# Tile 0 of x loaded on ScalarE's DMA queue in a fused attention and gated MLP kernel

## The chip, the cores and the metric

The kernel runs on one core of a Trainium2 chip. A core has TensorE (matmuls), VectorE, ScalarE and GpSimd (elementwise work and reductions), and SyncE, which here only issues DMAs. ScalarE can issue DMAs too, on a queue of its own. The metric is the time of one execution on the device, in microseconds (us); less is better.

## The reference

A block with two residual steps on x of shape 1 x 2048 x 448, in bf16:

```python
x = A_x
h = x + _A_ref(_layernorm(x), A_wqkv, A_w_phi, A_wo)
h2 = h + _B_ref(_layernorm(h), B_w_gate, B_w_up, B_w_down)

# _A_ref: 16 heads of 28
qkv = x @ wqkv                       # split into q, k, v by head
pq, pk = q @ w_phi, k @ w_phi        # one 28 x 28 matrix per head
phi_q = concat(softmax(pq), softmax(-pq)); phi_k likewise
kv = phi_k^T @ v;  z = sum of phi_k over the sequence
o = (phi_q @ kv) / (phi_q . z + 1e-6);  return o @ wo

# _B_ref: inner width 1792
return (sigmoid(x @ w_gate) * (x @ w_up)) @ w_down
```

The second input named x (B_x) is not used.

## The kernel before

The sequence is cut into 16 tiles of 128 rows; tile t of x holds rows n = t of every 16, so that each of the 128 partitions reads one run of 896 bytes per tile. A tile is normalized (bst: statistics, agg: mean and variance, pow1: the reciprocal root, xn: the normalized tile) and turned so that the model width lies on the partitions (xT: through TensorE for tiles 0 to 3, by a transposing DMA for the others). The per-head matrices w_phi are not applied to q and k: they are multiplied into the weights beforehand ("folds", w2m). For the fold of the key weights the kernel loads them in two halves (ld_k0 with row blocks 0 and 1, ld_k2 with 2 and 3), transposes each block on TensorE (wT0 to wT3), copies it out (wTe, the first two on ScalarE, the last two on VectorE), and multiplies it with Wphi, a matrix with the heads' blocks on its diagonal (w2m0, line 627). Wphi is cleared by VectorE (bd0, line 444) and then filled by four small DMAs on ScalarE's queue (wphi0 to wphi3), which wait for the clearing. Every fold reads all of Wphi. The folded weights are copied out by ScalarE (w2e0).

After that come the projections of keys and values per tile (pp and vv for pairs of the first four tiles, pv for one tile later), exponentials on ScalarE, the sums over the sequence, the query side, the output projection, the second normalization and the gated MLP, whose 14 blocks of inner width are interleaved with what is left of the attention.

The order of the work is written out by hand: for each engine a string of step names (ORDER, lines 243 to 312), which that engine runs strictly in this order. A step waits on semaphores for the steps on other engines that it depends on. For the step names that matter here the orders begin:

```
SyncE:   x1 x0 ld_k0 x2 ld_k2 x4 x6 ld_v0 x10 ld_v2 x8 x12 ld_q1 ...
ScalarE: wphi3 wphi2 wphi1 wphi0 kvzones wTe0 wTe1 xT1e xT0e w2e0_0 ...
TensorE: warm0 wT0 wT1 xT1 warm1 .. warm3 xT0 warm4 wT2 wT3 w2m0_0 warm5 w2m0_2 w2m0_1 w2m0_3 warm6 .. warm8 xT3 ppa0 ppb0 xT2 warm9 vva0 ...
VectorE: zero steps bd0 wopad0 wopad1 mask2 bst1 agg1 bst0 agg0 xn1 xn0 bst3 bst2 agg3 wTe2 agg2 wTe3 ...
GpSimd:  epsl0 v1ones neghalf epsr0 ident0 ident pow1_1 pow1_0 pow1_3 phipad nm1_3 xn3 pow1_2 pow1_4 xn2 ...
```

The "warm" steps are matmuls of zeros whose result nobody reads. x0 and x1 load one tile each (112 KB); the other names x2, x4, ... load two tiles each (224 KB). All plain loads are recorded at one line (439, the helper load), so the traces show them by their destination: x_sb, wk_sb, wv_sb, Wphi.

Of the kernel before, what the change touches and what calls it, by code (L numbers as in the profile page):

```python
# [18 lines left out]
class Graph:  # L19
# [109 lines left out]
    def emit(self, nc):  # L129
# [112 lines left out]

ORDER = {
# [6 lines left out]
    ),  # L250
    "act": (
# [103 lines left out]
def build(nc, A_x, A_wqkv, A_w_phi, A_wo, B_w_gate, B_w_up, B_w_down, out):  # L355
# [4 lines left out]
    x_t = A_x[0].rearrange("(p n) d -> p n d", p=P)  # L360
# [5 lines left out]
    with ExitStack() as es:  # L366
        def sb(name, shape, d=dt.bfloat16):
            return es.enter_context(nc.sbuf_tensor(name, shape, d))
# [5 lines left out]
        par = sb("par", [P, 2])  # L374
        st2 = sb("st2", [P, 2, 9], f32)
        mv2 = sb("mv2", [P, 2, 2], f32)
        x_sb = sb("x_sb", [P, NT, D])
# [60 lines left out]
        def load(name, dst, src, w, kb, r=(), eng="sp", many=None):  # L438
            return op(eng, name, lambda e: e.dma_start(dst, src), r=r, w=w, dma="in" if eng == "sp" else "ain",  # L439
                      nring=(48 if eng == "sp" else 8) if many is None else 0, kb=kb, many=many)  # L440
# [48 lines left out]


        def xload(a, b):
            return load("x%d" % a, x_sb[:, a:b, :], x_t[:, a:b, :], [("x", t) for t in range(a, b)], (b - a) * 112)

        def kload(a, b):
            load("ld_k%d" % a, wk_sb[:, a:b, :], A_wqkv[a * GP:b * GP, D:2 * D].rearrange("(kt p) n -> p kt n", p=GP),
# [13 lines left out]
        for a, b in ((0, 1), (1, 2), (2, 4), (4, 6), (6, 8), (8, 10), (10, 12), (12, 14), (14, 16)):  # L509
            xload(a, b)  # L510
# [95 lines left out]
        for kt in range(KT):  # L606
            b = (0, 1, 4, 5)[kt]
# [435 lines left out]
```

## Time and profile before

| what | value |
|---|---|
| time, median of 3 runs | 201.93 us (201.68 to 201.96) |
| the profiled execution: its time | 201.4 us |
| the profiled execution: its span | 199.5 us |
| granted TensorE clock over the span | 1.0 |
| busy: TensorE, VectorE, ScalarE, GpSimd | 98%, 64%, 50%, 35% of the span |
| chain that ended last, by engine | TensorE 92%, VectorE 3%, DMA 2%, SyncE's queue 1%, issue 1% |
| HBM read, written | 8.34 MB, 1.84 MB |

The span runs from the first to the last instruction of the core; the time around it belongs to the start and end of the execution. PE is TensorE's matmul row and PEld its weight loads, DVE is VectorE, ACT ScalarE, POOL GpSimd. SPq and ACTq are the rows of the DMA-issuing instructions of SyncE and ScalarE. L and a number is a line of the kernel. An arrow in a tile's name reads "written from": psum<-Wphi,WkT is a matmul of those two into PSUM.

### The profile page before, as it was taken

The numbers are of one execution on the slowest core, as the hardware profiler recorded it, in microseconds if no ns is written. First come the engines' busy times: TensorE is split into PE (matmuls) and PEld (weight loads), VectorE is DVE, ScalarE is ACT, GpSimd is POOL, SyncE is SP. The second block draws the span as 40 slices with busy tenths as digits, with TensorE's granted clock in tenths as the row PEclk, the third lists the DMA queues.
The fourth block names the chain that finished last, engine by engine and source line by source line (L and its number), as shares of the span: only waits on it lengthen the run. The fifth ranks groups of instructions, "written<-read, shape, count | busy, mean of one in ns | idle before, by whom it ended". The sixth has DMA issues, their size and how long they took to land.

```text
span 199.5 us, 5929 instructions
## 1 busy us (share of the span) xinstructions
PE 194.7 (98%) x2528; PEld 114.3 (57%) x2528; DVE 126.8 (64%) x309; ACT 100.0 (50%) x213; POOL 69.5 (35%) x107
## 2 busy tenths in 40 slices
PE   7999999999989999999999999999999999999995
PEld 2835555666557788886555444444555555555553
DVE  6999999978889876286558775246232522353224
ACT  3869899899795776356232443223323212222210
POOL 4689968733543456353303146100210000000000
DMA  6995925478941573213102204203020000003103
GB/s 153 341 128 124 86 56 133 114 228 275 347 60 34 135 114 55 53 37 75 40 17 64 58 3 92 43 0 97 3 53 3 0 0 3 0 0 96 45 3 92
DMA packets 32866, 16.26 MB, mean 82 GB/s; under 512 B 25096, under 2 KB 31944, under 8 KB 32840
## 3 DMA queue, kind: packets, MB, share of 16 engines
q1 hardware_dynamic: 32336, 15.86, 35.3%
q8 instruction: 20, 0.33, 0.7%
q10 hardware_dynamic: 504, 0.03, 0.2%
q14 instruction: 6, 0.05, 0.1%
HBM read 8.34 MB, written 1.84 MB: 51 GB/s over the span
## 4 chain that ended last, share of the span: by engine, by line
PE 92%; DVE 3%; DMA 2%; SPq 1%; issue 1%
PE psum L338 87%; PE psum L960 3%; DMA wk_sb<-in_A_wqkv_dram 2%; PE psum L627 1%; SPq L439 1%; PE psum L536 1%; DVE c_sb L808 1%; DVE st L833 1%; PE psum L550 0%; DVE b_sb L805 0%; DVE hn_pad L855 0%; DVE xnT L543 0%; PE psum L611 0%; DVE x_sb L835 0%; DVE rsm L802 0%
## 5 line engine op out<-in xcount | busy, mean ns | idle before, releaser
L338 PE MATMUL psum<-xnT,wg_sb 64*128 64x512 bf16 (+1 forms) x490 | 95.1, 333 | 0.3 <-DVE xnT L543 0.3
L338 PE MATMUL psum<-xnT,wu_sb 64*128 64x512 bf16 (+1 forms) x490 | 95.0, 333 | 0.1
L914 ACT ACTIVATE sg_sb<-psum 128x512 bf16<-128x512 f32 (+1 forms) x70 | 35.6, 515 | 75.6 <-PE psum L338 75.2
L920 DVE TENSOR_TENSOR hhT<-sg_sb,psum 128x512 bf16<-128x512 bf16 (+1 forms) x44 | 29.2, 674 | 46.6 <-ACT sg_sb L914 46.0
L338 PEld LDWEIGHTS psum<-xnT,wg_sb 64*128 64x128 bf16 x490 | 44.7, 94 | 20.3 <-DVE hhT L920 0.8
L338 PEld LDWEIGHTS psum<-xnT,wu_sb 64*128 64x128 bf16 x490 | 44.6, 94 | 14.0 <-PE psum L338 0.9
L338 PE MATMUL psum<-wd_sb,hhT 64*128 64x448 bf16 x392 | 43.8, 349 | 0.0
L338 PEld LDWEIGHTS psum<-wd_sb,hhT 64*128 64x128 bf16 x392 | 20.9, 94 | 16.8 <-DVE x_sb L840 0.3
L338 PE MATMUL psum<-wv_sb,xnT 64*128 64x448 bf16 x112 | 22.2, 351 | 0.1
L338 PE MATMUL psum<-Wk,xnT 64*128 64x448 bf16 x112 | 22.1, 350 | 0.1
L814 POOL TENSOR_TENSOR o_pad<-c_sb,rden 128x448 bf16<-128x448 bf16 x12 | 11.2, 935 | 26.5 <-DVE rden L810 26.0
L687 POOL TENSOR_TENSOR phi<-hhT,rs 128x896 bf16<-128x896 bf16 x10 | 16.9, 1704 | 2.9 <-DVE rs L683 1.7
L677 DVE TENSOR_REDUCE ss<-hhT 128x32 f32<-128x896 bf16 x16 | 17.0, 1063 | 0.3
L725 ACT ACTIVATE eq<-psum 120x1024 bf16<-120x1024 f32 x16 | 15.8, 1031 | 0.9 <-PE psum L338 0.9
L338 PE MATMUL psum<-xnT,Wq 64*120 64x512 bf16 x112 | 14.8, 384 | 0.1
L967 DVE SCALAR_TENSOR_TENSOR x_sb<-psum,x_sb 128x448 bf16<-128x448 f32 (+2 forms) x17 | 9.7, 594 | 7.5 <-PE psum L338 5.1
L919 ACT CAST xn_pad<-psum 128x256 bf16<-128x256 f32 x26 | 9.4, 375 | 6.4 <-PE psum L338 5.8
L338 PE MATMUL psum<-wo_o,oT 64*128 64x448 bf16 x49 | 11.5, 349 | 0.0
L338 PE MATMUL psum<-wo_e,oT 64*128 64x448 bf16 x49 | 11.5, 349 | 0.0
L920 POOL TENSOR_TENSOR hhT<-sg_sb,xn_pad 128x256 bf16<-128x256 bf16 x11 | 7.6, 694 | 11.1 <-ACT xn_pad L919 6.9
L338 PEld LDWEIGHTS psum<-Wk,xnT 64*128 64x128 bf16 x112 | 7.7, 94 | 5.5 <-PE psum L338 1.0
L805 DVE TENSOR_TENSOR b_sb<-psum,qq 128x464 bf16<-128x464 f32 x16 | 10.1, 634 | 0.7 <-PE psum L338 0.4
(112 smaller groups left out, 244.0 us busy)
## 6 DMA issues: line engine op xcount, KB each, us to landing
out_dram<-x_sb SPq DMA_DIRECT2D x15, 112.0 KB, 1.8
x_sb<-in_A_x_dram SPq DMA_DIRECT2D x7, 224.0 KB, 4.5
wd_sb<-in_B_w_down_dram SPq DMA_DIRECT2D x7, 224.0 KB, 7.5
wg_sb<-in_B_w_gate_dram SPq DMA_DIRECT2D x3, 448.0 KB, 4.5
wu_sb<-in_B_w_up_dram SPq DMA_DIRECT2D x3, 448.0 KB, 4.7
wv_sb<-in_A_wqkv_dram SPq DMA_DIRECT2D x2, 224.0 KB, 4.9
wk_sb<-in_A_wqkv_dram SPq DMA_DIRECT2D x2, 196.0 KB, 3.5
wo_e<-in_A_wo_dram SPq DMA_DIRECT2D x1, 336.0 KB, 3.2
```

The costliest lines, as they stand in the source:

```text
L338: p = e.matmul(o, lhsT=w, rhs=r, start=st, stop=sp, tile_position=(row, 0))
L439: return op(eng, name, lambda e: e.dma_start(dst, src), r=r, w=w, dma="in" if eng == "sp" else "ain", nring=(48 if eng == "sp" else 8) if ...
L677: op("dve", "ss%d" % t, lambda e: e.tensor_reduce(ss[:, s, :].rearrange("p (b h) -> p b h", h=2), eks.rearrange("p b (d h) -> p b h d", h= ...
L687: return e.tensor_tensor(phi[:, sp, :, :, :].rearrange("p b a n -> p (b a) n")[:, :, 0:56].rearrange("p b (d h) -> p b d h", h=2), eks.rea ...
L725: op("act", "eq%d_%d%s" % (c, i, "pm"[sg]), lambda e, sg=sg: e.activation(eq[c][:, sg, 2 * i:2 * i + 2, :].rearrange("p g n -> p (g n)"), ...
L805: op("dve", "b%d" % t, lambda e: e.tensor_tensor(h3(b_sb), OMv[:, :, :, 0:EV], h2(qq)[:, :, :, None].to_broadcast([P, NB, 8, EV]), ALU.mul ...
L814: return e.tensor_tensor(o_pad[:, t % NO, off:off + D].rearrange("p (h d) -> p h d", h=H), c_sb[:, t % NS, :, 0:DH], rden[:, t % NS, :][:, ...
L914: op("act", "sig" + nm, lambda e: e.activation(sg_sb[:, k, 0:N], bk(bg)[:, 0:N], ACT.Sigmoid), r=[B(bg)], w=[("sg", k)])
L919: op("act", "uc" + nm, lambda e: e.copy(up, bk(bu)[:, 0:N]), r=[B(bu)], w=[ub])
L920: op(("pool", "dve") if nm in UCOPY else "dve", "hh" + nm, lambda e: e.tensor_tensor(hhT[(t0 // 4) % NHH][:, ff, ns], sg_sb[:, k, 0:N], up ...
L960: p = e.matmul(bk(b)[:, lo:hi], lhsT=hb[:, ff, TS(t)], rhs=wd_sb[:, ff, lo:hi], start=ff == 0, stop=ff == FT - 1)
L967: op("dve", "fin%d%s" % (t, nm), lambda e: e.scalar_tensor_tensor(out=h_sb[:, t, lo:hi], in0=bk(b)[:, lo:hi], scalar=1.0, in1=h_sb[:, t, l ...
```

## The change

Step x0 is taken out of SyncE's order and put at the head of ScalarE's, ahead of the four Wphi loads. All other steps keep their order on every engine. The helper for x's loads passes on the engine that the order names, and a load that is not on SyncE uses ScalarE's set of semaphores.

```diff
 ORDER = {
     "sp": (
-        "x1 x0 ld_k0 x2 ld_k2 x4 x6 ld_v0 x10 ...
+        "x1 ld_k0 x2 ld_k2 x4 x6 ld_v0 x10 ...
     ),
     "act": (
-        "wphi3 wphi2 wphi1 wphi0 kvzones wTe0 ...
+        "x0 wphi3 wphi2 wphi1 wphi0 kvzones wTe0 ...
...
         def xload(a, b):
-            return load("x%d" % a, x_sb[:, a:b, :], x_t[:, a:b, :], [("x", t) for t in range(a, b)], (b - a) * 112)
+            return load("x%d" % a, x_sb[:, a:b, :], x_t[:, a:b, :], [("x", t) for t in range(a, b)], (b - a) * 112, eng=Graph.engine("x%d" % a))
```

18 rows, old and new, of the table ORDER are left out of this document.

## The prediction

> **What bounds the kernel now.** I read the page's busy times first, then the chain of waits in order of time, then the first 14 us of the timeline. The change touches only the loads at the start, so two things matter: what sets the pace after the start, and which wait at the start hands a delay on to it.
>
> ```profile
> PE 194.7 (98%) x2528; PEld 114.3 (57%) x2528; DVE 126.8 (64%) x309; ACT 100.0 (50%) x213; POOL 69.5 (35%) x107
> ...
> 0.72 0.39 SPq L439
> 1.18 0.41 SPq L439
> 1.64 0.42 SPq L439
> 2.10 0.46 SPq L439
> 2.60 3.82 DMA wk_sb<-in_A_wqkv_dram
> 6.47 0.62 PE psum L611 x8
> 7.09 0.20 PE psum L627 x4
> 7.29 0.45 PE psum L536 x8
> 7.73 0.59 PE psum L627 x12
> 8.32 1.12 PE psum L536 x20
> 9.44 0.22 PE psum L550 x4
> ...
> 63.72 55.53 PE psum L338 x800
> 119.30 72.45 PE psum L338 x706
> ```
>
> The columns of the chain are start, length and what the time went to. SyncE's first four issues (x1, x0, ld_k0, x2) stand on it, then the fifth, ld_k2, from its issue at 2.60 to its landing at 6.42; from 6.47 on TensorE runs piece on piece: the last weight transposes (L611), the folds (L627), warm-up matmuls (L536), xT3 (L550). The long later pieces have no wait inside. So whatever TensorE loses or gains by 10 us is still there at 199.5 us. x0 itself is not on the chain as a transfer, only as an issue of 0.41.
>
> **The neighbours of that chain.** The timeline's rows, start and length again, the idle time before it in brackets:
>
> ```profile
> 1.18 3.57 PE L536 MATMUL psum<-zero 128*128 128x512 bf16 x9 [1.18 <-DVE zero L443]
> 1.20 0.24 DVE L444 MEMSET Wphi<- 112x224 uint32 x1
> 1.47 1.90 ACTq L439 DMA_DIRECT2D Wphi<-in_A_w_phi_dram  x4
> 2.84 0.63 DVE L557 BATCH_NORM_STATS2 st<-x_sb 128x6 f32<-128x448 bf16 x1 [0.29 <-DMA x_sb<-in_A_x_dram]
> 3.09 0.93 SPq L439 DMA_DIRECT2D x_sb<-in_A_x_dram  x2
> 3.50 0.20 DVE L558 BATCH_NORM_AGGREGATE mv<-st 128x2 f32<-128x9 f32 x1
> 3.62 0.59 DVE L557 BATCH_NORM_STATS2 st<-x_sb 128x6 f32<-128x448 bf16 x1
> 4.76 0.62 PE L611 MATMUL psum<-ident,wk_sb 112*112 112x112 bf16 x8
> 6.47 0.62 PE L611 MATMUL psum<-ident,wk_sb 112*112 112x112 bf16 x8 [0.31 <-DMA wk_sb<-in_A_wqkv_dram]
> 6.88 0.25 PEld L627 LDWEIGHTS psum<-Wphi,WkT 112*128 112x128 bf16 x4
> 6.92 0.39 DVE L543 COPY WkT<-psum 112x448 bf16<-112x448 bf16 x1
> 7.52 0.65 PEld L627 LDWEIGHTS psum<-Wphi,WkT 112*128 112x128 bf16 x12
> 8.37 0.77 POOL L588 TENSOR_SCALAR xn_pad<-x_sb,nm,rst 128x512 bf16<-128x512 bf16 x1
> 9.28 0.39 PE L550 MATMUL psum<-ident,xn_pad 128*128 128x128 bf16 x4
> 10.34 2.26 POOL L588 TENSOR_SCALAR xn_pad<-x_sb,nm,rst 128x512 bf16<-128x512 bf16 x3
> 11.27 0.40 PE L550 MATMUL psum<-ident,xn_pad 128*128 128x128 bf16 x4
> ```
>
> Three strands meet on TensorE: the key weights (ld_k0, ld_k2), the four small Wphi loads that ScalarE issues and every fold needs, and the statistics of x on VectorE and GpSimd that end in xT3 and xT2.
>
> **The change part by part.**
>
> *x0 off SyncE.* One issue of 0.41 goes; with its gap, 1.18 to 1.64, every later SyncE entry up to the first wait on work is issued 0.46 earlier. ld_k0 gains nothing by that: the first transposes start at 4.76, just when the nine warm-up matmuls end (1.18 + 3.57 = 4.75). ld_k2 can gain at most the wait of 0.31 in front of the second transposes. That gain has cover over it: the third fold group's operand comes from the copy on VectorE at 6.92 (end 7.31), which stands in VectorE's own order behind the statistics, so of the loads at 7.52 no more than 0.2 is left; xT3 waits for the normalized tile on GpSimd (8.37 + 0.77 = 9.14, against 9.28), and xT2 for the first of three tiles (10.34 + 2.26/3 = 11.09, against 11.27). What is left at xT2 is below 0.18; less a hand-over of about 0.05 (ld_k2 lands at 6.42, TensorE starts at 6.47), I take 0.1. Value of this part alone: -0.1 us, bounds -0.2 and 0.
>
> *x0 onto ScalarE.* ScalarE's first work is the Wphi issue at 1.47, when the clearing of Wphi (1.20 + 0.24) is done. An issue there lasted
>
> ```profile
> L439 ACTq DMA_DIRECT2D Wphi<-in_A_w_phi_dram x4: 338/418/632, 1.5 to 3.0; - x4
> ```
>
> 338 to 632 ns. Begun at about 0.72, as on SyncE, x0's issue ends by 1.35 at the latest of these, ahead of 1.47. So ScalarE pays nothing: cover is the clearing of Wphi. Should the start be late or the issue over 0.75, the excess moves all four Wphi issues, one for one.
>
> *x0 beside x1.* x1's statistics start the moment x1 lands (2.84, idle 0.29 ended by the DMA). x0's start at 3.62, straight behind VectorE's own aggregate (3.50 + 0.20), so an earlier x0 is worth nothing. But its 112 KB now travel beside x1's rather than behind. The windows' rows end in the rate in GB/s:
>
> ```profile
> 2.00:2.50 0.50, 0.50 (x3) 0.22 (x2) 0.35 (x2) 0.00 (x0) 0.23 (x1) 1.00 0.81 226
> 7.50:9.50 2.00, 2.00 (x41) 1.99 (x38) 2.00 (x8) 1.85 (x5) 1.83 (x4) 1.00 1.08 368
> ```
>
> At 368 GB/s, 114,688 bytes take 0.31. So x1 lands 0 to 0.31 later; I take 0.2. All of the VectorE and GpSimd strand moves with it, up to xT3 and xT2, where it has about 0.1 of slack: on its own 0 to +0.2 at the end, best value +0.1. It runs parallel to the next part, so the larger counts, not the sum.
>
> *Wphi against the SyncE stream.* This is the term I forecast by. Wphi's loads carry 6.1 KB each, but what do they wait for? The second queue (q10) carries only them; the DMA view gives packets of the whole run, then of 0 to 3.38, 5.5 to 6.5 and 6 to 6.5 us, and then the landing time (last number, us after issue) of the two loads issued around the last Wphi, ld_k2 and x4:
>
> ```profile
> q10 hardware_dynamic: 504, 0.03, 0.2%
> ...
> q10 hardware_dynamic: 119, 0.01, 3.2%
> ...
> q10 hardware_dynamic: 47, 0.00, 3.1%
> ...
> q10 hardware_dynamic: 1, 0.00, 0.1%
> ...
> x_sb<-in_A_x_dram SPq DMA_DIRECT2D x1, 224.0 KB, 4.4
> wk_sb<-in_A_wqkv_dram SPq DMA_DIRECT2D x1, 196.0 KB, 3.8
> ```
>
> All Wphi issues are over at 3.37 (1.47 + 1.90). Yet 47 of 504 packets start after 5.5, one after 6.0: over two us in a queue of its own that has nothing else in it. The last Wphi (issued 3.0) therefore moves about in order of issue among SyncE's loads, between ld_k2 (issued 2.60, landed 6.42) and x4 (issued 3.09, landed 3.09 + 4.4 = 7.49). It must have landed by 6.88, when the first fold loads its weights without a wait of its own, so in 6.42 to 6.88.
>
> After the change SyncE is one slot ahead and ScalarE is not: x4 is issued at 2.60, in ld_k2's old place, and the last Wphi at 3.0 falls behind x4. It then lands about when x4 does: 7.49 less what the stream gains. That gain is 0 if the DMA engines are full from the first load on, 0.46 if the whole issue slot is won: 7.03 to 7.49. Between the ends I take the middle, 7.26, since the rate of 226 against 368 shows that the engines are neither idle nor full at 2 us. The first fold moves from 6.88 to 7.26, +0.38; bounds +0.15 and +0.61. Nothing absorbs it: from L627 at 7.09 to xT3 at 9.44 TensorE has piece on piece, then the key projections, whose results release ScalarE's exponentials. Late next are those, and VectorE's sums of them.
>
> The Trainium skill ("DMA: Bandwidth & Descriptors", "Queues, rings and completion order") says that each DMA engine takes turns between the queue rows that have work, a packet at a time. By that rule Wphi would not stand behind x4 and this term would be 0, leaving the first part's -0.1. The packets after 5.5 us do not look like turns taken with a queue that has little in it, so I go by them.
>
> *The rest.* xT4 onwards and the weight loads are issued on waits for other work or for TensorE, and follow TensorE; the four transposing loads ld_q start 0.46 earlier behind the same loads, and the folds for q that use them stand in TensorE's order behind the key projections. Cost nothing. SyncE's final waits count the same loads.
>
> *Sum.* Larger of +0.38 (fold) and +0.1 (x1), with the -0.1 gone because the fold, not ld_k2, now ends last: +0.38. The profiled execution took 201.4 around a span of 199.5; it becomes 199.88 and 201.8. It lies 0.53 under the median of the runs, 201.93; against that the forecast is 201.93 + 0.38 = **202.3 us**, slower by 0.19%.
>
> **Rivals.**
>
> *The fold does not wait (other side).* Place: the first fold at 6.88. If queues take turns, or ScalarE's issues go faster once x0 was first (632 falls to 338 and the last Wphi goes out at 2.7), Wphi lands by 6.88 and ld_k2's lead shows: 201.93 - 0.1 = 201.8, at best 0.31 + a little, 201.6. It decides once the last Wphi lands under 6.88. For it: two queues, 6.1 KB each. Against: the late packets. The rule of the Trainium skill's page named above would bring this case about.
>
> *x1 is held up and the fold is not.* x1 0.31 late, less 0.1 of slack: 202.1. For it: x1's landing is waited for at 2.84. Against: the rate of 226 leaves room.
>
> *Everything late together.* x0's issue starts late on ScalarE and pushes Wphi, or the stream gains nothing: +0.6 and more, 202.6 to 202.8. For it: the first ScalarE issue was the longest. Against: nothing precedes it there.
>
> *The change is hidden.* x1 unhurt, fold and GpSimd strand both at their old times: 201.9.
>
> **How the numbers follow.** Fold waits as forecast 0.50 (own range 202.0 to 202.6), everything late 0.12, x1 only 0.10, faster side 0.20, hidden 0.08. What a measurement of this kernel tells from no change is about 0.2%, 0.4 us: 201.53 to 202.33. Slower by more: about half of the first case, most of the second, and shares of tail, 0.42. Faster by more: only the end of the faster side, 0.12. The rest, 0.46. Range: 201.6 to 202.8, from the faster side's best to the late end, leaves out about 2 in 10.
>
> **What would show it.** In the changed profile: x0 as ScalarE's first DMA near 0.72; ld_k2 issued near 2.10 and x4 near 2.60; second-queue packets still moving after 6.5 us; a wait in front of L627 and its first weight load near 7.26; xT3 near 9.7 (9.28 + 0.38). Wrong if the first fold loads at 6.9 or before, if x1's statistics start much after 3.1, or if Wphi's first issue starts after 1.5. Wrong in the other way if the front moves as forecast and a later stage gives it back.

## The result and the profile after

The changed kernel takes 202.42 us (median of 16 runs, 202.14 to 202.88), the kernel before 201.83 us (median of 16, 201.43 to 202.59): 0.59 us or 0.29% slower, ratio 1.0029, 95% interval 1.0019 to 1.0039. The profiled execution of the changed kernel took 202.61 us with a span of 200.7 us, so it lies 0.19 above its median, while that of before lies 0.43 below its own (201.4 against 201.83). The gap of 1.2 us between the two traces is therefore twice the gap of the medians; causes have to be read from several traces.

The chain of waits of the changed kernel in order of time (start, length, what):

```profile
0.72 0.40 SPq L439
1.18 0.41 SPq L439
1.64 0.45 SPq L439
2.13 5.08 DMA wk_sb<-in_A_wqkv_dram
7.26 0.62 PE psum L611 x8
7.88 0.28 issue
8.15 0.36 PE psum L627 x4
8.51 0.45 PE psum L536 x8
9.55 1.12 PE psum L536 x20
10.67 0.22 PE psum L550 x4
...
64.93 55.53 PE psum L338 x800
120.51 72.45 PE psum L338 x706
```

One issue is gone from SyncE's part and ld_k2 goes out at 2.13 instead of 2.60, as announced. But its transfer takes 5.08 instead of 3.82: issued 0.47 earlier, it lands 0.79 later. A new gap of 0.28 stands ahead of the first fold (L627), and everything after is the old chain, moved by 1.2: the piece of 55.53 us began at 63.72 before and begins at 64.93 now. The middle and the end of the kernel neither gave anything back nor lost more.

The timeline's rows that answer to those of before:

```profile
0.72 0.41 ACTq L439 DMA_DIRECT2D x_sb<-in_A_x_dram  x1
1.47 1.88 ACTq L439 DMA_DIRECT2D Wphi<-in_A_w_phi_dram  x4
2.61 0.93 SPq L439 DMA_DIRECT2D x_sb<-in_A_x_dram  x2
3.50 0.63 DVE L557 BATCH_NORM_STATS2 st<-x_sb 128x6 f32<-128x448 bf16 x1 [0.96 <-DMA x_sb<-in_A_x_dram]
7.26 0.62 PE L611 MATMUL psum<-ident,wk_sb 112*112 112x112 bf16 x8 [0.44 <-DMA wk_sb<-in_A_wqkv_dram]
8.15 0.36 PE L627 MATMUL psum<-Wphi,WkT 112*128 112x112 bf16 x4 [0.28 <-DMA Wphi<-in_A_w_phi_dram]
11.08 2.27 POOL L588 TENSOR_SCALAR xn_pad<-x_sb,nm,rst 128x512 bf16<-128x512 bf16 x3
12.49 0.40 PE L550 MATMUL psum<-ident,xn_pad 128*128 128x128 bf16 x4
```

ScalarE issues x0 at 0.72 and Wphi at 1.47, unchanged. x1's statistics (L557) start at 3.50 instead of 2.84, with 0.96 of idle time that x1's DMA ended. The fold waits 0.28 for Wphi by name. xT2 stands at 12.49 instead of 11.27.

The windows show the transfers themselves: the last number is GB/s, the first pair the stretch. Before, then after:

```profile
2.00:2.50 0.50, 0.50 (x3) 0.22 (x2) 0.35 (x2) 0.00 (x0) 0.23 (x1) 1.00 0.81 226
2.50:3.50 1.00, 1.00 (x4) 0.38 (x3) 0.68 (x2) 0.10 (x1) 0.00 (x0) 1.00 0.95 211
3.50:5.00 1.50, 1.49 (x8) 0.51 (x7) 1.25 (x4) 1.48 (x2) 1.04 (x2) 1.00 0.99 278
```

```profile
2.00:2.50 0.50, 0.50 (x3) 0.22 (x2) 0.35 (x2) 0.00 (x0) 0.23 (x1) 1.00 0.64 143
2.50:3.50 1.00, 1.00 (x4) 0.39 (x3) 0.05 (x1) 0.12 (x1) 0.00 (x0) 1.00 1.13 351
3.50:5.00 1.50, 1.50 (x5) 0.53 (x4) 1.43 (x4) 1.46 (x2) 0.56 (x1) 1.00 0.98 188
```

With two loads going out together the first half microsecond moves less, 143 against 226, not more. The next one makes up for it, and from 3.5 to 5.0 the stream is slower again. Over the three microseconds together these rates come to about 0.70 MB against 0.74 before, so SyncE's lead brought no more bytes.

### The profile page after: what moved, and what is told of

Same layout as the page of the kernel before. It is cut to its first block, busy times and chain, and to the rows that moved or that the text cites. A ratio compares the mean times of both kernels' runs of the same rounds, so it can differ in the third digit from the quotient of the medians.

```text
span 200.7 us, 5929 instructions
## 1 busy us (share of the span) xinstructions
PE 195.6 (97%) x2528; PEld 114.3 (57%) x2528; DVE 126.9 (63%) x309; ACT 100.0 (50%) x213; POOL 69.6 (35%) x107
## 4 chain that ended last, share of the span: by engine, by line
PE 92%; DVE 3%; DMA 3%; issue 1%; SPq 1%
PE psum L338 86%; PE psum L960 3%; DMA wk_sb<-in_A_wqkv_dram 3%; PE psum L627 1%; PE psum L536 1%; SPq L439 1%; DVE c_sb L808 1%; DVE st L833 1%; PE psum L550 0%; DVE b_sb L805 0%; DVE hn_pad L855 0%; DVE xnT L543 0%; PE psum L611 0%; DVE x_sb L835 0%; DVE rsm L802 0%
```

## The experiments

The theory at the start was the forecast's: the last Wphi load falls behind x4, and the fold waits. Rival one: x1 is held up by x0 beside it. Rival two: the whole stream ran late in that trace by chance. The experiments stand in three groups, each with its own runs of the kernel before, with medians of 201.67, 201.70 and 201.78. In kernels with an added load, line numbers behind it are one higher (L612 is L611).

**The changed kernel twice more.** Nothing is altered.

> The changed kernel once more, unaltered, for a second trace and a time beside the kernel before. In the first two traces the first fold loaded its weights at 6.88 before and 8.12 after (+1.24), while the medians of the runs differ by 0.59 us. Theory (the last Wphi load lands behind x4, and the fold waits for it): the second trace shows the fold waiting again, its weight load between 7.2 and 8.1, and a shift at the end of the same size; time ratio 1.002 to 1.004. Rival one (x1 is held up by x0 beside it): x1's statistics start at 3.1 or later again and the fold is late because everything behind them is. Rival two (the whole stream of loads happened to run late in that one trace): x1's statistics start near 2.85 and the second half of the key weights lands before 6.4 this time.

> The changed kernel unaltered, a third trace. In the first the fold waited 0.28 for Wphi, in the second not at all; in both the key weights' second half landed at 7.2 to 7.4 although it was issued 0.47 earlier than before. If that lateness belongs to the change: it lands after 7.0 again and the first fold loads its weights after 7.6. If it was chance: it lands at 6.9 or before. The fold waits for Wphi or not, either way; ratio 1.002 to 1.005.

Measured: 202.35 us, ratio 1.0033 (1.0021 to 1.0045), and 202.29 us, ratio 1.0029 (1.0016 to 1.0041). Rows of the second trace's timeline, then of the third's:

```profile
3.58 0.63 DVE L557 BATCH_NORM_STATS2 st<-x_sb 128x6 f32<-128x448 bf16 x1 [1.03 <-DMA x_sb<-in_A_x_dram]
7.42 0.62 PE L611 MATMUL psum<-ident,wk_sb 112*112 112x112 bf16 x8 [0.53 <-DMA wk_sb<-in_A_wqkv_dram]
7.83 0.25 PEld L627 LDWEIGHTS psum<-Wphi,WkT 112*128 112x128 bf16 x4
```

```profile
3.56 0.63 DVE L557 BATCH_NORM_STATS2 st<-x_sb 128x6 f32<-128x448 bf16 x1 [1.02 <-DMA x_sb<-in_A_x_dram]
6.96 0.62 PE L611 MATMUL psum<-ident,wk_sb 112*112 112x112 bf16 x8
7.85 0.36 PE L627 MATMUL psum<-Wphi,WkT 112*128 112x112 bf16 x4 [0.27 <-DMA Wphi<-in_A_w_phi_dram]
```

x1's statistics start at 3.50, 3.58 and 3.56 in the three traces: that is the change and not chance, and rival two is out. The fold waits for Wphi in two of three, by 0.28 and 0.27; in the other, ld_k2 came so late (7.38 by the chain) that Wphi was there first. The fold's weights are loaded at 8.12, 7.83 and 7.82, against 6.88 in the first trace of the kernel before and 7.12 in the second, which follows. The third expectation left ld_k2 after 7.0 or by 6.9; it landed at about 6.95 (2.15 + 4.8), between the two.

**The kernel before once more.** Nothing is altered.

> The kernel before once more, unaltered, for a second trace of its first 14 us. If x1's landing at 2.82 is what this kernel does and not chance: x1's statistics start within 0.1 of 2.84, and the key weights' second half lands within 0.4 of 6.43. Ratio 0.999 to 1.001.

Measured: 201.86 us against 201.70, ratio 1.0008 (1.0000 to 1.0017). x1's statistics start at 2.86, ld_k2's transposes at 6.72 and the fold's weights at 7.12. The 0.25 between the two traces of one kernel has to do with TensorE: the nine warm-up matmuls took 3.57 in the first and 4.02 in the second, where TensorE then ran without a gap up to the fold. So 0.16 us is what two series of one kernel can differ by here, and the 0.5 to 0.7 us of the change is well above it.

**x4 back at its place.**

```diff
-        "x1 ld_k0 x2 ld_k2 x4 ...
+        "x1 ld_k0 x2 ld_k2 pad0 x4 ...
+        load("pad0", junk[:, 0, 0:64], x_t[:, 0, 0:64], [("junk", 0)], 16)
```

The small load of 16 KB takes a slot, so x4 and every SyncE load behind it goes out at its old time.

> The changed kernel with one more small load (16 KB) in SyncE's order between ld_k2 and x4, so that x4 is issued at its old place, near 3.05, behind the last Wphi; x0 stays on ScalarE. Theory: the last Wphi lands ahead of x4 again, the fold does not wait, and most of the loss goes: ratio to the kernel before 0.999 to 1.001. Rival one (x1 held up beside x0): nothing changes there, ratio stays 1.002 to 1.004, x1's statistics start after 3.1. Rival two: no change either.

Measured: 202.01 us, ratio 1.0016 (1.0007 to 1.0026), 0.34 under the changed kernel of the same group; the runs (201.82 to 202.29) barely touch its runs (202.26 to 202.61). That lies between the two expected ratios. Its chain:

```profile
0.72 2.86 DMA x_sb<-in_A_x_dram
...
3.60 0.64 DVE st L558
...
5.27 0.70 POOL rst L567
...
9.08 0.78 POOL xn_pad L589
...
9.90 0.40 PE psum L551 x4
```

ld_k2, issued at the same 2.13 as in the changed kernel, now takes 4.3 to land instead of 4.8 to 5.2, and the fold's weights are loaded at 7.12. No packet of Wphi moves after 6.5 us, although x0 still stands ahead of Wphi on ScalarE's queue; so that place alone does not make the fold wait. The chain has moved to the other strand: x1's landing, 2.86 after its issue, its statistics, GpSimd, xT3. So moving up x4 and what follows it is one cause, and x1 beside x0 stands behind it as a second.

**Only x0 beside x1, SyncE's other loads as before.**

```diff
-        "x1 ld_k0 x2 ld_k2 x4 ...
+        "x1 pad0 ld_k0 x2 ld_k2 x4 ...
```

> The changed kernel with the small load (16 KB) in x0's old place in SyncE's order, so that SyncE's loads from ld_k0 on are issued at the times of before, and only x0 beside x1 is left of the change. Theory: Wphi keeps its place between ld_k2 and x4, ratio 0.999 to 1.001. Rival one: x1 lands up to 0.31 later and the ratio stays at 1.001 to 1.003. Rival two: no forecast, within 0.2% of the changed kernel.

> The changed kernel with the small load in x0's old place once more: SyncE's other loads as before, only x0 beside x1 is left. The first time three of twelve runs were near 204.1 and the interval was wide (1.003 to 1.007), with the others about 202.2. If x0 beside x1 costs about what the first trace shows (x1's statistics 0.41 later): ratio 1.001 to 1.003, the statistics start after 3.1.

Measured: 202.27 us, ratio 1.0050 (1.0026 to 1.0074), and 202.37 us, ratio 1.0048 (1.0024 to 1.0073). In both series three of twelve runs were near 204, the others 201.94 to 202.81; these three pull the ratios up, out of every range that was expected; the medians alone give 1.0030 and 1.0029. x1's statistics start at 3.25 and 3.43. The second trace is of one of the runs near 204 (204.04 us). The loss is there without SyncE's lead, but its size can't be read from this pair: the added load delays ld_k0 as well (3.6 and 4.1 to land in the two traces, 3.1 and 3.4 before), which brings in the slow matmuls of this document's last section.

**Without Wphi, both kernels.** The four loads, and the waits on them, are left out, so Wphi stays zero.

> The changed kernel without its four Wphi loads: Wphi stays zero, so the folded weights are zero and the output is not the reference's; all other work is done. Theory: the fold has nothing to wait for but the key weights, which now land earlier, so the time falls below that of the changed kernel by 0.4 us or more. The four small loads also slow the stream (about 280 GB/s while they move against 368 after), so the time can fall below the kernel before as well: ratio 0.996 to 0.999. Rival one: x1's statistics still start after 3.1 and hold xT3 and xT2; the ratio stays above 1.001.

> The kernel before without its four Wphi loads (Wphi stays zero, so the output is not the reference's), as a pair to the changed kernel without them, which took 202.10 against 201.67. If x1 beside x0 is the main cause, the gap remains: this one takes 201.4 to 201.7 and x1's statistics start at 2.84. If Wphi's place behind x4 were the main cause, the two without Wphi would be alike within 0.2 us.

Measured: the changed kernel without Wphi 202.10 us, ratio 1.0022 (1.0009 to 1.0035); the kernel before without it 201.66 us, ratio 0.9996 (0.9987 to 1.0005). With no Wphi to wait for, 0.4 us of the change's cost remains, and x1's statistics start at 3.66 in the one and 2.86 in the other. The chain of the first begins, as with x4 back, with x1's landing. The forecast that the time falls under that of before is wrong. Against the changed kernel, leaving out Wphi saves 0.25, with intervals that overlap; against the kernel before, nothing. From 3.5 to 5.0 the first moves 187 GB/s and the second 330, so the slow stretch of the changed kernel is not Wphi's doing. In all traces in which x0 starts with x1 this rate is 187 to 239, in all others 278 to 330.

**Wphi issued earlier.**

```diff
-        "zero steps bd0 ...
+        "bd0 zero steps ...
```

> The changed kernel with Wphi cleared before the 'zero' tile in VectorE's order, so that ScalarE issues the four Wphi loads about 0.25 earlier (near 1.2) and the last one stands at about x4's issue, no longer 0.33 behind it. The warm-up matmuls start 0.25 later. If the fold's wait for Wphi, the term of the forecast, carries a good part of the loss: the median falls by 0.15 or more below the changed kernel's 202.35 to 202.42, and the fold does not wait. If it carries little (in the second trace of the changed kernel the fold went straight behind the last transposes), the time stays within 0.1 of it.

Measured: 201.99 us, ratio 1.0014 (1.0004 to 1.0025), 0.30 under the changed kernel of the same group; eight of its twelve runs lie below the lowest run there (202.12). Wphi is issued from 1.18, the fold does not wait for it (weights at 7.42, straight behind the transposes at 7.01). In the changed kernel's trace of that group the transposes begin at 6.96 and the weights only at 7.82. ld_k2 came no sooner, so by these two traces the gain is the fold's wait, and not a faster stream.

**A second queue that starts with x1, almost without bytes.**

```diff
-        "wphi3 wphi2 wphi1 wphi0 kvzones ...
+        "pad0 wphi3 wphi2 wphi1 wphi0 kvzones ...
+        load("pad0", junk[0:16, 0, 0:64], x_t[0:16, 0, 0:64], [("junk", 0)], 2, eng="act")
```

> The kernel before with one 2 KB load at the head of ScalarE's order, x0 left on SyncE: a second queue starts together with x1, with almost no bytes. If x1 is late because x0's bytes share the DMA engines: x1's statistics start within 0.05 of 2.84 and the ratio is 0.999 to 1.001. If it is late because two queues make their first accesses at the same moment: the statistics start at 3.1 or later and the ratio is 1.001 to 1.003.

Measured: 201.81 us, ratio 1.0007 (0.9995 to 1.0020). Both issues go out at 0.72 and 0.73, and x1 lands on time:

```profile
0.72 0.42 ACTq L439 DMA_DIRECT2D junk<-in_A_x_dram  x1
0.73 0.87 SPq L439 DMA_DIRECT2D x_sb<-in_A_x_dram  x2
2.89 0.63 DVE L558 BATCH_NORM_STATS2 st<-x_sb 128x6 f32<-128x448 bf16 x1 [0.35 <-DMA x_sb<-in_A_x_dram]
```

So a second queue that starts at the same moment does not by itself delay x1; the load of 112 KB does. Whether its bytes or its number of packets matter is not told apart.

**x0 on ScalarE, but behind x1.** One wait is added.

```diff
-PACE = {"ld_wg0": "pvb15", "ld_wg1": "kva14"}
+PACE = {"x0": "zero", "ld_wg0": "pvb15", "ld_wg1": "kva14"}
```

> The changed kernel with one wait more: x0 on ScalarE waits for VectorE's first clearing (done at 1.11 us), so that it is issued near 1.15, where SyncE issued it before, and x1 has its first 0.4 us alone. SyncE stays one slot ahead. The first four runs left two causes: x1 lands 0.4 to 0.8 late beside x0 (x1's statistics at 3.25 to 3.66 instead of 2.84), and x4 moved up delays the key weights and Wphi (with x4 put back, the median fell from 202.35 to 202.01). If the start beside x1 is the larger cause: x1's statistics start within 0.1 of 2.84 and the ratio falls to 1.000 to 1.002. If the place of x4 is the larger: x1 is back at 2.84 but the fold still loads its weights at 7.2 or later and the ratio stays at 1.002 to 1.004.

Measured: 202.03 us, ratio 1.0019 (1.0003 to 1.0035). x1 is back:

```profile
1.15 0.41 ACTq L439 DMA_DIRECT2D x_sb<-in_A_x_dram  x1
2.87 0.63 DVE L557 BATCH_NORM_STATS2 st<-x_sb 128x6 f32<-128x448 bf16 x1 [0.32 <-DMA x_sb<-in_A_x_dram]
```

and 0.33 us over the kernel before are left, about what the other single repair left, with a wide interval (0.06 to 0.71 us). Wphi's first issue moves from 1.47 to 1.59 here. The chain of this trace has no load on it:

```profile
1.17 4.02 PE psum L536 x9
5.19 0.75 PE psum L611 x8
5.94 0.43 PE psum L550 x4
...
7.72 0.20 PE psum L627 x4
```

TensorE has piece on piece from the warm-up to the fold, and was slow up to 7 us (0.63 for four matmuls of L550). ld_k2 landed at 6.93, still later than in the kernel before (6.42 and 6.71), but TensorE came to its transposes only at 7.12. The ratio lies where the first expectation put it, the fold's weights (7.51) where the second did, and what is left is not the place of x4 alone.

**Both repairs together.** The wait for x0 and the small load ahead of x4.

> The changed kernel with both suspected causes taken away: x0 on ScalarE waits for VectorE's first clearing, so that it is issued near 1.15 behind x1, and the small load (16 KB) in SyncE's order puts x4 back behind the last Wphi. Each alone left 202.0 against 201.7. If the two causes (x1 beside x0; x4 moved up) carry the loss together, this one is at the kernel before: ratio 0.999 to 1.001, x1's statistics at 2.9 or earlier, the key weights' second half landed by 6.7. If a third cause is left, such as x0 itself landing late beside ld_k0 (3.90 with the wait alone, against 3.25), the ratio stays at 1.001 or above and the second statistics start after 3.8.

Measured: 201.81 us against 201.78, ratio 0.9997 (0.9982 to 1.0012). x1's statistics start at 2.83, the second transposes at 6.60, xT2 at 11.56. The loss is gone within that interval, with x0 still on ScalarE's queue and still landing late enough for its statistics to start at 4.07. The expectation's third cause is not there in the time. Single repairs leave 0.34 and 0.33, together they leave 0.03, and the change costs 0.5 to 0.7 in the three series. That these numbers add up does not yet show two delays in a row; the next table tells how they meet.

How the front sets the end, from the timelines and the spans:

| kernel | x1's statistics | x0's statistics | fold's weights | xT2 on TensorE | span |
|---|---|---|---|---|---|
| before | 2.84 | 3.62 | 6.88 | 11.27 | 199.5 |
| before, again | 2.86 | 3.63 | 7.12 | 11.52 | 199.7 |
| both repairs | 2.83 | 4.07 | 7.13 | 11.56 | 199.7 |
| before, second queue with 2 KB | 2.89 | 4.12 | 7.14 | 11.61 | 199.8 |
| before, without Wphi | 2.86 | 4.11 | 7.40 | 11.80 | 200.0 |
| only x0 beside x1 | 3.25 | 4.03 | 7.44 | 11.83 | 200.0 |
| Wphi earlier | 3.55 | 4.32 | 7.42 | 11.84 | 200.0 |
| x4 back | 3.60 | 4.38 | 7.12 | 11.90 | 200.1 |
| x0 behind x1 | 2.87 | 3.92 | 7.51 | 11.90 | 200.1 |
| changed, without Wphi | 3.66 | 4.43 | 7.23 | 11.95 | 200.2 |
| changed, third | 3.56 | 4.34 | 7.82 | 12.20 | 200.4 |
| changed, second | 3.58 | 4.36 | 7.83 | 12.22 | 200.4 |
| changed, first | 3.50 | 4.28 | 8.12 | 12.49 | 200.7 |
| only x0 beside x1, again | 3.43 | 4.20 | 8.63 | 13.89 | 202.1 |

In every row the span ends 188.1 to 188.3 after xT2 starts: the front alone sets the time. In all rows but the last, xT2 comes 4.37 to 4.40 after the fold's weights, or 7.49 to 7.52 after x0's statistics (the second tile of VectorE's order), whichever is later. So there are two strands, and the later one counts. In the three traces of the change it is the fold; x0's statistics alone would give 11.8 to 11.9. With x4 back the fold is as early as in the kernel before, and the strand of x1 and x0 comes out from behind it.

No experiment points to a kernel faster than both: the three that come nearest to the kernel before, both repairs, the kernel before without Wphi and that with the 2 KB load, are equal to it within their intervals.

## Why the prediction was right, and where it was not

The direction, the place (the first 12 us, carried to the end one for one) and the time, 202.3 forecast against 202.42 measured, came out. The working behind it did so in parts only. The change itself was forecast at +0.38 and measured at +0.59; the time comes nearer than that because the forecast stood on the median of three runs, 201.93, and sixteen runs give 201.83. One of the forecast's own signs of being wrong came, too: x1's statistics start at 3.50, much after 3.1.

*x0 off SyncE* was valued at -0.1, with ld_k2 landing earlier. ld_k2 was issued 0.45 to 0.48 earlier in every trace and landed 0.2 to 1.0 later (7.21, 7.38 and 6.95 against 6.42 and about 6.71). A lead in issue was taken for a lead in arrival. From 3.5 to 5.0 the stream moved 188 GB/s against 278, but from 2.5 to 3.5 it had moved more, 351 against 211; from 2 to 5 us the three traces moved about 0.70, 0.72 and 0.76 MB against 0.74 and 0.75 in the two of before. The stream as a whole was thus hardly slower. Why ld_k2 in particular lands later is not shown.

*x0 onto ScalarE* costs nothing there: right. Its issue took 0.41 from 0.72, and Wphi went out at 1.47 as before.

*x0 beside x1* is the term that was mis-sized. It was bounded by 0 and 0.31, from the bytes of x0 at the rate of the full stream, and taken at 0.2 and, less slack, 0.1 at the end. Measured, x1 lands 0.64 to 0.74 later in the three traces of the change. The bound assumed that two loads together move at the rate of a stream well under way, 368; from 2.0 to 2.5 us the core moved 143, 185 and 165 with both, 226 and 240 with one behind the other. With x4 put back, this strand alone costs 0.34 at the end. The forecast also saw x0's bytes act on this strand alone; but in the one trace with x0 behind x1 the stream from 3.5 to 5.0 is back at 309, and the fold is earlier than in the three traces of the change.

*Wphi against the SyncE stream*, the term forecast by, is real. Packets of Wphi move after 6.5 us, where none was before; the second queue from 6.5 to 7.6 in the first trace of the change:

```profile
q10 hardware_dynamic: 27, 0.00, 1.7%
```

The fold waited in two of three traces, the first fold moved by 0.70 to 1.24 against the two traces of before (forecast 0.38), and Wphi's own part of that is 0.27 or 0.28 where it shows. The rest is ld_k2, which the forecast had arriving earlier, and TensorE's own start. Repairs of this part give back 0.34 (x4 back) and 0.30 (Wphi earlier), close to the 0.38; but x4 back also brought ld_k2 0.5 to 0.9 sooner, so that its 0.34 is not Wphi's alone. That Wphi stands still behind x4, as the forecast had it, the packets do not show: in the first trace of the change the second queue moved 185 from 3.4 to 4.5, 130 to 5.5, 132 to 6.5 and 27 to 7.6, beside SyncE's. By the rule of the Trainium skill ("DMA: Bandwidth & Descriptors", "Queues, rings and completion order") that queues take turns, as the forecast used it, this term would be 0, and the fold's waits say that it is not. The rule itself is not refuted by that, since both queues moved packets all the time; how the turns are dealt is not shown.

*The sum* took the larger of two parallel terms, and by the table that step is right: xT2 follows the later strand. Both strands were priced too low, the fold at +0.38 and x1 at +0.1. That the two repairs seem to add follows without a sum: with x4 back the fold strand falls behind the other one, and x0 behind x1 brings both strands forward. How much of the fold's delay comes from x4 and how much from x0 beside x1 is open, for the repairs' intervals are as wide as the shares.

*Rivals.* That the fold does not wait and all is faster did not happen. x1 held up did happen, at twice its price. "Everything late together", priced at +0.6 and more, is nearest in size to the +0.59; its place, a late first issue on ScalarE, is wrong, its second half, a stream that gains nothing, right. Terms wrong by several tenths, a base 0.1 too high and traces of before that were faster than their medians met in one number, and part of its closeness is luck. The number was better than its working.

## What to carry to other kernels

An issue slot saved on a queue is worth something only if the transfer behind it also lands earlier, so read issue and landing apart. Where the first load of a kernel starts a chain that reaches the end, leave it alone on the DMA engines: here a second full load started with it delayed it by 0.4 to 0.8 us, a 2 KB one by 0.05 at most. Moving one queue ahead also moves it past the loads of the other queue, and a small load that a fold needs can then land too late. Where two strands meet, put back one cause at a time and both together, and read in each trace which strand came last.

## What the runs showed of the hardware

Two loads of 112 KB that start together were slower to land than the same two 0.46 us apart: x1's statistics start at 3.50 to 3.58 instead of 2.84 and 2.86, with the rate from 2.0 to 2.5 us at 143, 185 and 165 GB/s in the three traces against 226 and 240 in the two of before. What in the transfer path does this was not tried.

TensorE's pace at the start differs between runs of one kernel: the nine warm-up matmuls took 3.57 in the first trace of before and 4.02 in the second. In the kernel with the small load in x0's place, the one run near 204 that has a trace lost its 2 us there. The chain of its first trace (a run of 201.94):

```profile
7.85 0.45 PE psum L537 x8
8.30 0.59 PE psum L628 x12
```

and of its second (a run of 204.04):

```profile
1.64 4.12 DMA wk_sb<-in_A_wqkv_dram
5.80 0.99 PE psum L612 x8
9.30 0.85 PE psum L537 x8
10.15 0.79 PE psum L628 x12
```

The same warm-ups and folds took 0.85 and 0.79 instead of 0.45 and 0.59: TensorE was at a lower pace until about 10 us, after it had stood idle for 0.60 waiting for ld_k0. The Trainium skill ("TensorE: Matmul & The Clock Gate", "Part 1: The HAM clock gate (the "warmup" mystery)") says that the clock starts at half rate and is released after a window of sustained work that runs free of the kernel's start. The durations agree with that; the granted clock in the profile's rows stayed at 1.00 in these stretches, so they don't show it. The idle time alone is not the reason: the first trace has 0.68 of it at the same place and is fast behind it. There the nine warm-up matmuls had taken 3.44, in the second trace 4.02. Whether the idle 0.60 behind the longer warm-up caused the late release was not tried by itself.
